# Attention plus token mixer on one core: the softmax sums inverted by way of DRAM, with a new order of score tiles and gelu steps

## The chip, the cores and the metric

The kernel runs on one core of a Trainium2 chip. TensorE (PE) multiplies matrices, VectorE (DVE), ScalarE (ACT) and GpSimd (POOL) work on tiles, and SyncE (SP) issues nearly all DMAs. The metric is the device time in microseconds. "us" below is microseconds.

## The reference, cut to what matters

`x` has 2048 rows and 640 columns. The attention part has 32 heads of 20 columns that share one key and one value matrix. The mixer part works across the rows. A gate per row mixes both.

```
g = sigmoid((x * gate_w).sum(-1, keepdims=True))
q = (x @ wq) in 32 heads of 20;  k = x @ wk;  v = x @ wv
p = softmax(q k^T * 20**-0.5);   a = concat_heads(p @ v) @ wo
h = layernorm(x)
u = gelu(einsum("bsd,sf->bdf", h, w1) + b1)      # F = 1728
b = (einsum("bdf,fs->bds", u, w2) + b2)^T
out = g * a + (1 - g) * b
```

All of it is float32. The kernel keeps the precision by splitting operands into a high and a low part in TensorE's fp32r format and adding three products (high times high, high times low, low times high).

## The kernel before, in words

**Units.** The attention is cut into 32 groups (`NU`), numbered n: four blocks of 512 query rows by eight groups of four heads. Each group has 16 units, one per block of 128 keys. For a unit TensorE makes four score tiles (128 keys by 512 queries, line 702, called "s" here), ScalarE takes the exponential of each (line 711) into a `p` tile, and four matmuls (line 737) multiply the `p` tiles by the values `v_sb`, one head to each 32 rows of one accumulator. The value tile is 20 columns of v and 12 columns of ones, so rows 20 to 31 of each 32-row block of the accumulator hold the softmax sums.

**Row maxima.** Before the exponentials of a group may start, the maximum of each query row must be known. TensorE makes the scores a second time, turned (line 490, called "m"), and VectorE reduces each 128x512 tile to one column (line 496). A group needs 64 m tiles, 32 in each row half of TensorE. The maxima go through a DRAM scratch (lines 523 and 530) into two extra rows of the query tile `qst`. The next group's `qmx` tile is fetched by `new_qmax` (lines 159 and 142: six DMAs) when both halves have started a new group (line 501).

**Stretches.** `main` (line 1085) writes out one stretch: s and m tiles (512 columns, "X") and mixer or projection matmuls (320 columns, "F") on the two row halves of TensorE at the same time, then the value matmuls of two units (`pv_group`, line 727) with the full array. In one half run about 16 X tiles, in the other 15 to 24 F matmuls and one to three X. The two halves change places with each stretch. A group is eight stretches. A table `PATTERN` (line 1060), keyed by the count of F matmuls, gives the order of s and m in the half with the X tiles, and what stands before and after the F matmuls in the other. `share` (line 1068) spreads the m tiles over the stretches: it takes one out of every fourth stretch of the first stage while the table would give more than are needed, and later divides what is left in proportion to the table.

There are three stages of stretches, called here the w1 stage (82 stretches of 24 F, line 993; one more before it fills the pipe), the w2 stage (128 stretches of 20 or 21 F, line 805) and the wo stage (32 stretches of 15 F, line 938). A lead of 46 m tiles per half stands before them and 26 units stand behind them (the tail), where no m tile is left.

**Banks.** Seven PSUM banks serve s, m and the value accumulator. `bank_take` and `bank_give` (lines 456 and 460) choose banks with a small clock of estimated engine times (`USE`, `busy`), which decides the order of the instructions when the program is built.

**The end of a group.** After each pair of units ScalarE copies the accumulator out (line 749), GpSimd adds it to `sums[0]` (line 750). When a group ends (line 751), a list `later` gets steps that `settle` (line 1049) runs one at a time: once in the middle of each stretch, once at its end. A step marked True runs at ends only, unless all row maxima are done (`spare`). Before the change the steps are: `scale` (VectorE turns the 32x32 blocks of `on` into `ot`, line 763, takes the reciprocals of the sums, line 769, and GpSimd multiplies, line 770), `back` (VectorE turns the result back, line 777), `high` (line 780) and `low` (line 783) on GpSimd with eight DMAs of the result to `o_scr` (line 787).

**Queues.** SP issues DMAs in program order and stops at one whose semaphore is not there. Eight DMA semaphores take turns, so a DMA also waits for the eighth before it.

**gelu.** `gelu` (line 534) puts its steps on a list `chain`, of which `settle` runs one at each call (`pop_chain`). In the last line of it (594) are the steps of the 21 columns that run in the w1 stage: `square` on ScalarE, `cube_p` on GpSimd, an empty step, `tanh` on ScalarE, `prod_p` and `high_p` on GpSimd.

**Early loads.** `tail_load(i)` (line 857) fetches rows of `o_scr` and `y_scr` for the tail; line 1042 says in which of the last stretches the first eight are issued.

Of the kernel before, what the change touches and what calls it, by code (L numbers as in the profile page):

```python
# [9 lines left out]
F32 = mybir.dt.float32  # L10
F32R = mybir.dt.float32r
# [6 lines left out]
P = 128  # L18
S, D, H, DH, F = 2048, 640, 32, 20, 1728
# [5 lines left out]
NB = 512  # L25
NQB = S // NB
NQ = H // 4
NU = NQB * NQ
# [12 lines left out]
def mix_kernel(ctx: ExitStack, tc: tile.TileContext, A_x, A_wq, A_wk, A_wv, A_wo,  # L41
               B_x, B_w1, B_b1, B_w2, B_b2, gate_w, out):
    nc = tc.nc
# [9 lines left out]
    o_scr = dram.tile([2, D, S], F32, name="o_scr")  # L53
    y_scr = dram.tile([S, D], F32, name="y_scr")
    m_scr = dram.tile([NU, P, 32], F32, name="m_scr")

    ident = const.tile([P, P], F32, name="ident")
    make_identity(nc, ident)
# [112 lines left out]
    with tc.tile_pool(name="pa", bufs=1) as pa, \  # L171
# [222 lines left out]
        for sb in range(NQB):  # L394
# [11 lines left out]
            for m in range(DC):  # L406
                turned = []
# [59 lines left out]
    def busy(engine, us):  # L467
        clock[engine] = max(clock[engine], clock["now"]) + us
# [65 lines left out]
    def gelu(d, fc, accs):  # L534
        both = fin.tile([P, D], F32, name="yo")
        xg, t1 = both[:, :HD2], both[:, HD2:]
        hi, lo = u_hi[d][:, fc, :], u_lo[d][:, fc, :]
        busy("act", 0.43)
        nc.scalar.activation(xg, accs[0][:, :HD2], AF.Identity, bias=bias[:, NS + fc:NS + fc + 1])

        def square():
            busy("act", 0.38)
            nc.scalar.activation(t1, xg, AF.Square)

        def add():
            nc.vector.tensor_add(xg, xg, accs[1][:, :HD2])  # L546
            square()

        def tanh():
            busy("act", 0.37)  # L550
            nc.scalar.activation(t1, t1, AF.Tanh, scale=GC * 0.044715)

        def high():
            nc.scalar.activation(hi, t1, AF.Copy)

        def low():
            nc.gpsimd.tensor_sub(lo, t1, f32(hi))

        def cube_p():
            nc.gpsimd.tensor_scalar(t1, t1, 1.0, 1.0 / 0.044715, op0=ALU.mult, op1=ALU.add)  # L560
            nc.gpsimd.tensor_mul(t1, t1, xg)

        def prod_p():
            nc.gpsimd.tensor_scalar(t1, t1, 1.0, 1.0, op0=ALU.mult, op1=ALU.add)
            nc.gpsimd.tensor_mul(t1, t1, xg)

        def plus(c):
            nc.scalar.activation(t1, t1, AF.Copy, bias=c)

        def mul():  # L570
            nc.gpsimd.tensor_mul(t1, t1, xg)

        def cubed():
            add()
            plus(1.0 / 0.044715)

        def tanh_plus():
            tanh()
            plus(1.0)

        def high_p():
            nc.gpsimd.tensor_copy(hi, t1)
            nc.gpsimd.tensor_sub(lo, t1, f32(hi))

        if len(accs) == 2:
            ends, ahead[:] = list(ahead), [high, low]
            if fc == PRO - 1:
                add()
                chain.extend((*ends, cube_p, None, tanh, prod_p, high_p))
            else:  # L590
                chain.extend((*ends, *[None] * (2 - len(ends)), cubed, None, None, mul, *[None] * 4, tanh_plus,
                              None, mul, None, None, None))
        else:
            chain.extend((square, cube_p, None, tanh, prod_p, high_p))

    def pop_chain():
        f = chain.pop(0) if chain else None
# [127 lines left out]
    later = []  # L725

    def pv_group(us, keep=False):
        n, kb = units[us[0]]
        assert units[us[-1]][0] == n
        if not otile:  # L730
            otile.append(bank_take())
        o = otile[0]
        opened = not keep or kb == 0 or us[0] == len(units) - TAIL
        ends = kb + len(us) == NS
        for i, u in enumerate(us):
            for hh in range(4):
                nc.tensor.matmul(o[32 * hh:32 * hh + 32, :], v_sb[:, kb + i, :], ptiles.pop((u, hh)),  # L737
                                 start=opened and i == 0, stop=(i == len(us) - 1) and (ends or not keep),
                                 skip_group_check=True)
        if not keep:  # L740
            begin = max(clock["act"], clock["pv"] + 0.14)
            clock["act"] = begin + 0.477
            pool.append((begin + 0.65, otile.pop()))
            if kb == 0:
                sums[0] = ev.tile([P, NB], F32, name="acc", bufs=2)
                nc.scalar.activation(sums[0], o, AF.Copy)
            else:
                part = ev.tile([P, NB], F32, name="part", bufs=2)
                nc.scalar.activation(part, o, AF.Copy)  # L749
                nc.gpsimd.tensor_add(sums[0], sums[0], part)  # L750
        if ends and n < NU - 1:
            qb, g = divmod(n, NQ)
            ot = ev.tile([P, NB // 32, 32], F32, name="ot")
            rl = ev.tile([P, NB // 32], F32, name="rl")
            on = sums[0]
            oh, ol = ot.rearrange("p c e -> p (c e)").bitcast(F32R), on.bitcast(F32R)
            direct = spare[0]
            if keep:
                nc.vector.tensor_add(on, on, o)

            def turn():
                busy("dve", 0.65)
                nc.vector.transpose(ot.rearrange("p c e -> p (c e)"), on)

            def scale():
                if not direct:
                    turn()
                busy("dve", 0.17 if not spare[0] else 0.87)
                nc.vector.reciprocal(rl, ot[:, :, DH])
                (nc.vector if spare[0] else nc.gpsimd).tensor_mul(ot, ot, rl[:, :, None].to_broadcast([P, NB // 32, 32]))  # L770

            if direct:
                turn()

            def back():
                busy("dve", 0.65)
                nc.vector.transpose(on, ot.rearrange("p c e -> p (c e)"))

            def high():
                nc.gpsimd.tensor_copy(oh, on)  # L780

            def low():
                nc.gpsimd.tensor_sub(ol, on, f32(oh))
                for j, t in enumerate((oh, ol)):
                    for hh in range(4):
                        r = (4 * g + hh) * DH
                        nc.sync.dma_start(out=o_scr[j, r:r + DH, qb * NB:(qb + 1) * NB],
                                          in_=f32(t[32 * hh:32 * hh + DH, :]))

            if direct:  # L790
                later.append((False, None))
            later.extend(((True, scale), (True, back), (False, high), (False, low)))

    def b2_jobs(st):
        hold = {}
# [243 lines left out]
    assert sum(visits) == len(units) - TAIL  # L1039
    early = NS - 4 - NA + 4  # L1040
    for i in range(early):
        ph[len(ph) - 3 - 2 * (early - 1 - i)][1].append(lambda i=i: tail_load(i))


    for i, (st, r0, _) in enumerate(jobs):
# [3 lines left out]
    def settle(wide=False):  # L1049
        for _ in range(2 if spare[0] else 1):  # L1050
            if later and (wide or spare[0] or not later[0][0]):
# [5 lines left out]
    sent, back_in = {0}, {0}  # L1057

    AHEAD, DRAIN, ENTER, FIRST = 4, 0.19, 0.138, 0.1
    PATTERN = {24: ("smssmsmmssmssmmm", "Fm"), 20: ("smsmssmmsmmssm", "mFs"), 21: ("smsmsmmssmmsmsm", "Fs"),  # L1060
               15: ("smsssmmmssms", "mFs"), 0: ("mmmmmmmmmmssss", "Fsmm")}

    def pattern(k):
        return PATTERN[len(ph[k][0]) if visits[k] else 0]
# [237 lines left out]
```

## Time and profile before

| | us |
|---|---|
| median of 3 runs (lowest to highest) | 1632.41 (1632.35 to 1633.01) |
| the profiled execution, own time | 1631.96 |
| its span in the profile | 1630.2 |
| DVE busy, share of the span | 1400.5, 86% |
| ACT busy, share of the span | 1297.2, 80% |
| POOL busy, share of the span | 858.5, 53% |
| row maxima on DVE, lines 496 on s and ms banks | 566.1 and 535.9 |
| transposes on DVE, lines 763 and 777, 31 each | 21.8 each |

The span begins with the first instruction that counts and ends with the last; 1.8 us of the run's time lie outside. PE and PEld are TensorE's matmuls and its weight loads. Matmuls of the two row halves overlap in time, and several matmuls are in flight at once, so durations on PE add up to more than passes. In the views of instructions the first column is the start, the second the duration, and "x16" means that rows of the same kind were merged. On DVE and ACT too an instruction starts before the one ahead of it has left: the distance of two starts, and not the duration, is what one costs.

### The profile page before, as it was taken

The numbers are of one execution on the slowest core, as the hardware profiler recorded it, in microseconds if no ns is written. First come the engines' busy times: TensorE is split into PE (matmuls) and PEld (weight loads), VectorE is DVE, ScalarE is ACT, GpSimd is POOL, SyncE is SP. The second block draws the span as 40 slices with busy tenths as digits, with TensorE's granted clock in tenths as the row PEclk, the third lists the DMA queues.
The fourth block names the chain that finished last, engine by engine and source line by source line (L and its number), as shares of the span: only waits on it lengthen the run. The fifth ranks groups of instructions, "written<-read, shape, count | busy, mean of one in ns | idle before, by whom it ended". The sixth has DMA issues, their size and how long they took to land.

```text
span 1630.2 us, 39380 instructions
## 1 busy us (share of the span) xinstructions
PE 1622.6 (100%) x14877; PEld 1127.8 (69%) x14877; DVE 1400.5 (86%) x2404; ACT 1297.2 (80%) x2567; POOL 858.5 (53%) x974
## 2 busy tenths in 40 slices
PE   9999999999999999999999999999999999999998
PEld 7899766766676667666666666666666666666666
DVE  6689999999999999999999999899999999777723
ACT  4445778787887878888888888888888888999975
POOL 6568666767686767544544344354444432433400
PEclk9999999999999999999999999999999999999999
DMA  7655222322233223222212222222222112335421
GB/s 213 210 164 146 71 73 68 74 70 76 70 81 80 63 63 83 57 65 73 65 51 59 58 60 49 73 65 73 65 65 65 54 44 58 95 101 184 133 74 41
DMA packets 173603, 135.88 MB, mean 83 GB/s; under 512 B 32793, under 2 KB 139446, under 8 KB 173414
## 3 DMA queue, kind: packets, MB, share of 16 engines
q1 hardware_dynamic: 173126, 133.04, 29.6%
q8 instruction: 117, 1.92, 0.5%
q14 instruction: 72, 0.59, 0.1%
q10 hardware_dynamic: 288, 0.33, 0.1%
HBM read 100.27 MB, written 31.65 MB: 81 GB/s over the span
## 4 chain that ended last, share of the span: by engine, by line
PE 99%; ACT 0%; DVE 0%; issue 0%; DVEq 0%; ACTq 0%
PE ms L737 14%; PE g L805 11%; PE s L737 11%; PE s L702 9%; PE g L993 9%; PE ms L702 8%; PE ms L490 7%; PE s L490 7%; PE o L737 5%; PE pp L298 4%; PE pu L623 3%; PE o L702 3%; PE o L490 2%; PE g L938 2%; PE ml L490 1%; PE s L893 1%
## 5 line engine op out<-in xcount | busy, mean ns | idle before, releaser
L496 DVE TENSOR_REDUCE mp<-ms 128x1 f32<-128x512 f32 x859 | 566.1, 683 | 69.7 <-PE ms L490 61.9
L496 DVE TENSOR_REDUCE mp<-s 128x1 f32<-128x512 f32 x810 | 535.9, 682 | 44.1 <-PE s L490 37.9
L711 ACT ACTIVATE p<-s 128x512 f32<-128x512 f32 x906 | 534.2, 624 | 37.8 <-PE s L737 13.1
L711 ACT ACTIVATE p<-ms 128x512 f32<-128x512 f32 x847 | 498.3, 621 | 36.7 <-PE s L737 11.4
L750 POOL TENSOR_TENSOR acc<-acc,part 128x512 f32<-128x512 f32 x212 | 274.4, 1294 | 392.9 <-ACT part L749 373.9
L702 PE MATMUL s<-qst,kst 62*128 62x512 f32 x906 | 353.8, 413 | 0.0
L702 PE MATMUL ms<-qst,kst 62*128 62x512 f32 x847 | 335.5, 413 | 0.4 <-ACT p L711 0.4
L490 PE MATMUL ms<-kst,qmx 60*128 60x512 f32 x859 | 332.6, 410 | 0.3 <-ACT p L711 0.3
L490 PE MATMUL s<-kst,qmx 60*128 60x512 f32 x810 | 316.4, 409 | 0.6 <-DVE yo L546 0.5
L993 PE MATMUL g<-slot,wh 64*128 64x320 f32 x1344 | 306.8, 313 | 0.0
L993 PEld LDWEIGHTS g<-slot,wh 64*128 64x128 f32 x1344 | 221.5, 184 | 68.7 <-DVE mp L496 35.2
L129 POOL TENSOR_TENSOR wl<-wr,wh 128x512 fp32r<-128x512 f32 (+1 forms) x176 | 217.7, 1237 | 29.4 <-ACT wh L126 9.7
L737 PE MATMUL ms<-p,v_sb 128*32 128x512 f32 x1904 | 228.9, 598 | 0.0
L496 DVE TENSOR_REDUCE mp<-o 128x1 f32<-128x512 f32 x287 | 196.0, 683 | 20.5 <-PE o L490 18.3
L993 PE MATMUL g<-slot,wl 64*128 64x320 f32 x672 | 206.4, 307 | 0.0
L702 PEld LDWEIGHTS s<-qst,kst 62*128 62x128 f32 x906 | 166.7, 185 | 55.1 <-ACT p L711 31.7
L805 PE MATMUL g<-u,wh 64*128 64x320 f32 x864 | 196.7, 310 | 0.0
L805 PE MATMUL g<-slot,wh 64*128 64x320 f32 x864 | 196.3, 309 | 0.0
L702 PEld LDWEIGHTS ms<-qst,kst 62*128 62x128 f32 x847 | 156.2, 185 | 55.3 <-ACT p L711 43.0
L737 PE MATMUL s<-p,v_sb 128*32 128x512 f32 x1536 | 184.7, 598 | 0.0
L711 ACT ACTIVATE p<-o 128x512 f32<-128x512 f32 x280 | 174.1, 622 | 11.5 <-PE ms L737 5.5
L490 PEld LDWEIGHTS ms<-kst,qmx 60*128 60x128 f32 x859 | 157.5, 185 | 9.2 <-ACT p L711 3.3
(244 smaller groups left out, 3158.0 us busy)
## 6 DMA issues: line engine op xcount, KB each, us to landing
wr<-in_B_w_dram SPq DMA_DIRECT2D x136, 256.0 KB
qmx<-q_scr SPq DMA_DIRECT2D x192, 80.0 KB
qst<-q_scr SPq DMA_DIRECT2D x192, 80.0 KB
y_scr<-yo SPq DMA_DIRECT2D x16, 320.0 KB
slot<-o_scr SPq DMA_DIRECT2D x16, 320.0 KB
o_scr<-ot SPq DMA_DIRECT2D x124, 40.0 KB
o_scr<-acc SPq DMA_DIRECT2D x124, 40.0 KB
q_scr<-qh SPq DMA_DIRECT2D x19, 256.0 KB
```

Source lines behind the costliest of these rows:

```text
L129: nc.gpsimd.tensor_sub(wl[:, :nv], wr[:, :nv], f32(wh[:, :nv]))
L298: nc.tensor.matmul(pp, w, t, start=first and n == 0, stop=not more and n == len(steps) - 1)
L490: nc.tensor.matmul(ms, qmax[n][64 * b:64 * b + 60, pr, qt * P:(qt + 1) * P], kst[64 * b:64 * b + 60, kq * NB:(kq + 1) * NB], start=True, s ...
L496: r = nc.vector.tensor_reduce(mtiles[n][:, c, kq:kq + 1], ms, axis=AX.X, op=ALU.max)
L623: nc.tensor.matmul(pu[r][:, :HD2], w[rows, c, :], h[rows, st, :], start=(st == 0 and k == 0), stop=(st == NS - 1 and k == 2))
L702: nc.tensor.matmul(s, kst[64 * b:64 * b + 62, kb * P:(kb + 1) * P], q[64 * b:64 * b + 62, pr, :], start=True, stop=True)
L711: e = nc.scalar.activation(p, s, AF.Exp, scale=SCALE)
L737: nc.tensor.matmul(o[32 * hh:32 * hh + 32, :], v_sb[:, kb + i, :], ptiles.pop((u, hh)), start=opened and i == 0, stop=(i == len(us) - 1) a ...
L750: nc.gpsimd.tensor_add(sums[0], sums[0], part)
L805: other_tile(half, nc.tensor.matmul(hold["p"][:, :HD2], w[r, i, :], u[d][r, fc, :], start=(hold["n"] == 1), stop=(hold["n"] == 6 * FC - 3)))
L938: other_tile(half, nc.tensor.matmul(hold["p"][:, :HD2], o[r, c, :], w[r, c, d * HD2:(d + 1) * HD2], start=(hold["n"] == 1), stop=(hold["n" ...
L993: other_tile(half, nc.tensor.matmul(hold["p"][:, :HD2], w[r, st % HS, :], h[d][r, st, :], start=(hold["n"] == 1), stop=(hold["n"] == 6 * NS)))
```

## The change

The reciprocals of the sums no longer come from turned tiles. Seven steps replace `scale`, `back`, `high` and `low`, and each runs at the next call of `settle`, at ends and in the middle: `sums_out` (four DMAs of one 2 KB row each, the sums of four heads, to a new DRAM scratch `l_scr`), `sums_in` (one DMA that brings 4 x 512 sums back as 128 rows of 16), `inverse` (VectorE, 128x16, and one DMA of the result to `l_scr`), `inverse_in` (four DMAs, each one head's 512 reciprocals repeated to 32 rows, into `ot`), `scale` (GpSimd multiplies `on` by that in place), then `high` and `low` as before. The one group that ends in the tail with `keep` still uses the two transposes. The table for 24 and for 15 F matmuls is replaced; the one for 15 has four m where it had five. The gelu of the w1 stage waits one more step before `tanh`. The last four of the early loads are issued up to three stretches later.

```diff
+    l_scr = dram.tile([2, NU, 4, NB], F32, name="l_scr")
...
-            chain.extend((square, cube_p, None, tanh, prod_p, high_p))
+            chain.extend((square, cube_p, None, None, tanh, prod_p, high_p))
...
             on = sums[0]
-            oh, ol = ot.rearrange("p c e -> p (c e)").bitcast(F32R), on.bitcast(F32R)
-            direct = spare[0]
+            flat = ot.rearrange("p c e -> p (c e)")
+            oh, ol = flat.bitcast(F32R), on.bitcast(F32R)
             if keep:
                 nc.vector.tensor_add(on, on, o)
 
-            def turn():
-                busy("dve", 0.65)
-                nc.vector.transpose(ot.rearrange("p c e -> p (c e)"), on)
+            def turned():
+                nc.vector.transpose(flat, on)
+                nc.vector.reciprocal(rl, ot[:, :, DH])
+                nc.vector.tensor_mul(ot, ot, rl[:, :, None].to_broadcast([P, NB // 32, 32]))
+
+            def back():
+                nc.vector.transpose(on, flat)
+
+            def sums_out():
+                for hh in range(4):
+                    r = 32 * hh + DH
+                    nc.sync.dma_start(out=l_scr[0, n, hh:hh + 1], in_=on[r:r + 1, :])
+
+            def sums_in():
+                nc.sync.dma_start(out=rl, in_=l_scr[0, n].rearrange("h (r c) -> (h r) c", r=32))
+
+            def inverse():
+                busy("dve", 0.17)
+                nc.vector.reciprocal(rl, rl)
+                nc.sync.dma_start(out=l_scr[1, n].rearrange("h (r c) -> (h r) c", r=32), in_=rl)
+
+            def inverse_in():
+                for hh in range(4):
+                    nc.sync.dma_start(out=flat[32 * hh:32 * hh + 32, :],
+                                      in_=l_scr[1, n, hh:hh + 1].to_broadcast([32, NB]))
 
             def scale():
-                if not direct:
-                    turn()
-                busy("dve", 0.17 if not spare[0] else 0.87)
-                nc.vector.reciprocal(rl, ot[:, :, DH])
-                (nc.vector if spare[0] else nc.gpsimd).tensor_mul(ot, ot, rl[:, :, None].to_broadcast([P, NB // 32, 32]))
-
-            if direct:
-                turn()
-
-            def back():
-                busy("dve", 0.65)
-                nc.vector.transpose(on, ot.rearrange("p c e -> p (c e)"))
+                nc.gpsimd.tensor_mul(on, on, flat)
...
-            if direct:
-                later.append((False, None))
-            later.extend(((True, scale), (True, back), (False, high), (False, low)))
+            first = (None, turned, back) if keep else (sums_out, sums_in, inverse, inverse_in, scale)
+            later.extend((False, f) for f in (*first, high, low))
...
-        ph[len(ph) - 3 - 2 * (early - 1 - i)][1].append(lambda i=i: tail_load(i))
+        ph[len(ph) - (17 - 2 * i if i < early - 4 else 6 + early - 4 - i)][1].append(lambda i=i: tail_load(i))
...
-    PATTERN = {24: ("smssmsmmssmssmmm", "Fm"), 20: ("smsmssmmsmmssm", "mFs"), 21: ("smsmsmmssmmsmsm", "Fs"),
-               15: ("smsssmmmssms", "mFs"), 0: ("mmmmmmmmmmssss", "Fsmm")}
+    PATTERN = {24: ("msmsmmssmsmmsmss", "Fm"), 20: ("smsmssmmsmmssm", "mFs"), 21: ("smsmsmmssmmsmsm", "Fs"),
+               15: ("smsmssmsmss", "mFs"), 0: ("mmmmmmmmmmssss", "Fsmm")}
```

## The prediction

> **What bounds the kernel now.** I read the head of the page first, then busy time by stage, then the timeline of single stretches, engine by engine. The profiled execution took 1631.96 us, of which the span is 1630.2; the median of the three runs, 1632.41, lies 0.45 above it.
>
> ```profile
> span 1630.2 us, 39380 instructions
> ...
> PE 1622.6 (100%) x14877; PEld 1127.8 (69%) x14877; DVE 1400.5 (86%) x2404; ACT 1297.2 (80%) x2567; POOL 858.5 (53%) x974
> ...
> PE 99%; ACT 0%; DVE 0%; issue 0%; DVEq 0%; ACTq 0%
> ```
>
> TensorE is the bound by both its busy share and the chain. But a matmul that waits for a bank counts as busy, so this says which engine, not how much could go. The Trainium skill ("Trainium Kernel Development and Optimization", Performance Expectations) says the same, that matmul busy time is a bad measure and weight-load busy time a good one; by it the 69% of PEld would leave much room. The timeline of the stretches shows less room than that.
>
> The windows are the three stages of stretches (82, 128 and 32 of them):
>
> ```profile
> core 0: us, PE busy (x) PEld busy (x) DVE busy (x) ACT busy (x) POOL busy (x), PEclk, DMA share, GB/s
> 170.70:665.70 495.00, 494.42 (x4662) 344.00 (x4658) 461.61 (x774) 396.43 (x801) 352.61 (x417) 1.00 0.28 72
> 665.70:1384.40 718.70, 718.35 (x6695) 480.65 (x6691) 652.99 (x1106) 612.10 (x1186) 317.62 (x348) 1.00 0.23 61
> 1384.40:1546.50 162.10, 162.10 (x1444) 103.11 (x1440) 124.65 (x211) 152.75 (x304) 66.56 (x72) 1.00 0.43 130
> ```
>
> A stretch costs 495.0/82 = 6.04 us, 718.7/128 = 5.61 us and 162.1/32 = 5.07 us. Next the end of one stretch of the wo stage, on PE:
>
> ```profile
> 1437.53 0.39 PE L490 MATMUL s<-kst,qmx 60*128 60x512 f32 x1
> 1437.61 0.46 PE L702 MATMUL ms<-qst,kst 62*128 62x512 f32 x1
> 1437.87 0.49 PE L702 MATMUL s<-qst,kst 62*128 62x512 f32 x1
> 1438.29 0.64 PE L737 MATMUL ms<-p,v_sb 128*32 128x512 f32 x4
> ```
>
> The X tile at 1437.61 is the last of the half that has the F matmuls. The one at 1437.87 is the twelfth of the other half, and the value matmuls start 0.42 us behind it. So the half with the X tiles sets the end here. And VectorE in the w2 stage, at the end of a group:
>
> ```profile
> 695.45 0.69 DVE L496 TENSOR_REDUCE mp<-ms 128x1 f32<-128x512 f32 x1 [0.83 <-PE ms L490]
> ...
> 700.25 0.70 DVE L763 STREAM_TRANSPOSE ot<-acc 128x512 f32<-128x512 f32 x1
> 700.98 0.25 DVE L769 RECIPROCAL rl<-ot 128x16 f32<-128x16 f32 x1
> 701.23 0.69 DVE L496 TENSOR_REDUCE mp<-s 128x1 f32<-128x512 f32 x1
> ...
> 703.03 0.68 DVE L496 TENSOR_REDUCE mp<-s 128x1 f32<-128x512 f32 x1
> 703.63 0.68 DVE L496 TENSOR_REDUCE mp<-ms 128x1 f32<-128x512 f32 x1
> ...
> 706.02 0.70 DVE L777 STREAM_TRANSPOSE acc<-ot 128x512 f32<-128x512 f32 x1
> ```
>
> Reductions start 0.60 us apart without a break, and between stretches VectorE has one gap (0.83 us of idle time in the first row). The transposes sit in that gap.
>
> **The change part by part.**
>
> *The transposes go.* They cover 0.70 us each, two for each of 30 groups, all in the gap just shown. What is late next without them is again the first m tile of the next stretch. So I count their removal at 0; bounds: 0, and 30 x 2 x 0.60 = 36 us if they were on the path, which the 0.83 us of idle time excludes in the w2 stage.
>
> *Fewer m tiles in the wo stage.* The built program's order has five m where it had six in 21 of the 32 stretches. Of these tiles 18 move to the w1 stage (all 82 stretches have nine, where 18 had eight), one ahead of it, two to the w2 stage. Without its twelfth X tile the one half ends at 1437.53, the other at 1437.61, and the value matmuls can start at 1437.61 + 0.42 = 1438.03, 0.26 earlier. What would be late next is ScalarE, which has as many exponentials as before:
>
> ```profile
> 1433.53 0.59 ACT L952 ACTIVATE yo<-g,g_col 128x320 f32<-128x320 f32 x1
> 1433.94 1.16 ACT L711 ACTIVATE p<-s 128x512 f32<-128x512 f32 x2
> ...
> 1436.23 0.61 ACT L711 ACTIVATE p<-ms 128x512 f32<-128x512 f32 x1
> 1436.71 1.11 ACT L711 ACTIVATE p<-s 128x512 f32<-128x512 f32 x2
> ```
>
> Two starts are 0.48 apart, and line 952 takes 0.41 in every second stretch: 9 x 0.48 + 0.41/2 = 4.53 us in a stretch of 5.07 - 0.26 = 4.81. It fits, but with 4.73 in the stretches that have line 952. I take 0.23 instead of 0.26: 21 x 0.23 = **-4.8 us** (bounds -5.5 and 0).
>
> *The w1 stage.* Starts of the value matmuls of six stretches in a row, the last from another window:
>
> ```profile
> 235.28 1.92 PE L737 MATMUL ms<-p,v_sb 128*32 128x512 f32 x16
> 241.76 1.92 PE L737 MATMUL s<-p,v_sb 128*32 128x512 f32 x16
> 247.77 1.92 PE L737 MATMUL o<-p,v_sb 128*32 128x512 f32 x16
> 253.82 1.92 PE L737 MATMUL s<-p,v_sb 128*32 128x512 f32 x16
> 259.87 1.92 PE L737 MATMUL ms<-p,v_sb 128*32 128x512 f32 x16
> ```
> ```profile
> 265.80 1.50 PE L737 MATMUL s<-p,v_sb 128*32 128x512 f32 x12
> ```
>
> Nine m tiles cost 6.01 to 6.05 us. The first distance, 6.48 us, and the last, 5.93, are stretches of eight; in the first the last m tile waited for a bank. If every stretch took 6.00, the stage would take 492.0, 3.0 less than now. The new table starts with an m, which gives VectorE its first tile one X earlier, and ends in "smss" and not in "mmm", so that fewer banks hang on VectorE when the value matmuls need one. Against that, the nine reductions fill 9 x 0.60 = 5.4 of 6.0 us in each stretch now, and the reciprocal (0.25) stands amid them. I take half: **-1.5 us** (bounds -3.0, and +1.3 if nothing but the 18 added tiles counts, at 6.00 - 5.93 = 0.07 each). The extra gelu step moves `tanh` half a stretch away from `cube_p`, and lies in a chain of eight half stretches; 0.
>
> *The sums through DRAM.* In the w2 stage the built order puts this on SP: four stores of sums, then the **six DMAs of the next `qmx`**, then `sums_in`. VectorE's `inverse` stands behind the fourth reduction of the second stretch after the group's end. All times from T, the first matmul after the group's value matmuls:
>
> ```profile
> 694.89 0.49 PE L702 MATMUL s<-qst,kst 62*128 62x512 f32 x1
> ```
> ```profile
> 695.81 1.29 POOL L750 TENSOR_TENSOR acc<-acc,part 128x512 f32<-128x512 f32 x1 [4.41 <-ACT part L749]
> ```
> ```profile
> 237.57 0.34 SPq L523 DMA_DIRECT2D m_scr<-mt  x1
> 239.30 2.74 SPq L530 DMA_DIRECT2D qst<-m_scr  x4
> ...
> 704.79 2.28 SPq L142 DMA_DIRECT2D qst<-q_scr  x6
> ```
> ```profile
> GB/s 213 210 164 146 71 73 68 74 70 76 70 81 80 63 63 83 57 65 73 65 51 59 58 60 49 73 65 73 65 65 65 54 44 58 95 101 184 133 74 41
> ```
>
> The sum is complete at 697.10, T + 2.2. Four stores at 0.34: SP is free at T + 3.6. The six loads take 2.28 to issue: `sums_in` goes out at T + 5.9. How long it takes to land no row tells. A store of 16 KB is done 239.30 - 237.57 = 1.73 us after its issue (SP waited for it to read it back), which gives T + 7.6 as the lower end. In front of it in the DMA queue stand 6 x 80 KB, 2.25 us at the 213 GB/s of the first slice; if they start to move only when `sums_in` is issued, it lands at T + 9.9. They start up to 2.3 us earlier, so I take T + 8.4, nearer to the lower end. VectorE wants it when the fourth reduction is over, at 703.63, T + 8.7. So VectorE doesn't wait, with 0.3 us to spare. What it would cost: `inverse` would hold the reductions behind it, their banks, and TensorE that waits for these banks. I count **+1.5 us** for the w2 stage, 16 groups x 0.1: the reciprocal's 0.25 now stands amid reductions and no longer in the gap (bounds: 16 x 1.2 = +19 if it lands at T + 9.9, and -2.4, since transpose and reciprocal, 0.98 us together, overran the gap of 0.83 by 0.15 in each group). In the other stages no `qmx` loads stand between (but for two groups), and it lands at T + 2.2 + 1.4 + 2 x 1.73 = T + 7.1 or before, ahead of the middle of the second stretch.
>
> *SP's queue.* SP now stands at the store of the reciprocals until VectorE has run (T + 9.0), and at `inverse_in` for that store (1.73 more). Behind them are two weight loads, a `qst` fetch and the fetch of the maxima. Weights are fetched far ahead, as SP's own waits show, since it stands there for GpSimd to free a buffer; the other two are for the next group, some stretches off: 0.
>
> ```profile
> SPq L110 <- POOL wl L129: 413.1, 29, 28.1
> ```
>
> *Behind the reciprocal.* Its store, `inverse_in` behind up to six loads, and `scale` on GpSimd follow. GpSimd may stand there for some us. It idled 4.41 us before the addition above, its next work is due a stretch later, and nobody waits for `o_scr` until later stages: 0; if it were late, ScalarE's copy of the accumulator two stretches on would wait, at most the 1.3 us of one addition in each group.
>
> *The early loads* move behind the stores that they read; 0.
>
> Sum: -4.8 - 1.5 + 1.5 = -4.8, of 1631.96 that is 1627.2; with the 0.45 to the median **1627.6 us**, 0.3% faster.
>
> **The rivals.**
>
> 1. *VectorE waits for the sums* (slower). The mechanism is the six loads between `sums_out` and `sums_in`; the place is `inverse` in 16 groups of the w2 stage; it decides from T + 8.7 on. For it: 0.3 us of margin on a landing that no row shows. Against it: the loads ahead have two microseconds of head start. Price at a landing of T + 9.6: 16 x 0.9 = +14 against the +1.5 above, so 1640. Beyond 0.2% slower from about 0.6 us of wait. Chance 0.20. The Trainium skill ("DMA: Bandwidth & Descriptors", Specifications) says that pieces below 512 B are read, modified and written; the 64-byte pieces of `sums_in` and of the inverse's store are such. The nearest row, the store of 128-byte pieces above, took 1.73 us; no run here shows 64.
> 2. *The m tiles only change their place.* The wo stage stays at 5.07 since ScalarE, at 4.73 of 4.81, and not the X tiles, sets its end (0), the w1 stage lies between -1.5 and +1.3, the w2 stage at +1.5: 1632.4 to 1635.2, say 1633. For it: ACT busy 152.75 of 162.10 there. Chance 0.20.
> 3. *It gives more than the forecast.* Every stretch of the w1 stage at 6.00 (-3.0), wo at -5.5, the w2 stage -2.4: 1632.4 - 10.9 = 1621.5. For it: VectorE gets the gap back in all stages. Against it: the w2 stage has hardly a stretch that shows it missing. Chance 0.10.
> 4. *The change doesn't do what it says*: the transposes still run, since `keep` groups use them. Only one group is such. Chance 0.
>
> **How the numbers follow.** Forecast 0.50, rivals 0.20, 0.20, 0.10. The range reaches from the third rival, 1621.5, to the first with 0.65 us of wait, 1637; beyond lie about 0.15 on the upper and 0.04 on the lower side. 0.2% is 3.3 us, about what a measurement of this kernel can tell from no change. Faster than 1629.1: most of the forecast (0.46) and rival 3, 0.56. Within: 0.04 of the forecast and most of rival 2, 0.21. Slower than 1635.7: rival 1 and the rest, 0.23.
>
> **What would show it.** Stretches of five m tiles in the wo stage at 4.8 to 4.85 us (right) or 5.0 and more (rival 2). The w1 stage at 492 to 495. In the w2 stage no idle time of VectorE before its new reciprocal; if "DMA" appears there as the releaser with over 0.5 us a time, rival 1 holds and the stage is longer than 720. GpSimd waiting at `scale`, without a trace on PE. The forecast fails where the landing is misjudged, or where another of TensorE's waits for banks comes up under the new table.

## The result, and the profile after

| | us |
|---|---|
| before, median of 4 runs beside it (lowest to highest) | 1632.38 (1632.18 to 1633.01) |
| after, median of 4 runs (lowest to highest) | 1625.18 (1623.61 to 1627.24) |
| ratio, 95% interval | 0.9956 (0.9944 to 0.9969) |
| profiled execution of after, own time and span | 1627.24 and 1625.4 |

The kernel is faster by 7.2 us, 0.4%. The forecast was 1627.6, in the range and 2.4 us too high. The changed kernel's runs differ by 3.6 us, those of before by 0.8, and the profiled execution is the slowest of the four. In after, lines from 490 to 760 are numbered one higher than before (L703 is the s tile, L491 m, L497 its reduction, L738 the value matmul); L773 stores the sums, L776 loads them, L780 is the new reciprocal, L781 its store, L785 loads the repeated rows, L789 is GpSimd's multiply, and the F matmuls of the three stages are L1004, L816 and L949.

The head of the page of after, busy times and chain:

```profile
span 1625.4 us, 39511 instructions
...
PE 1616.6 (99%) x14877; PEld 1127.4 (69%) x14877; DVE 1351.8 (83%) x2344; ACT 1311.0 (81%) x2567; POOL 866.6 (53%) x974
...
PE 97%; DMA 1%; SPq 1%; DVE 1%; ACT 0%; POOL 0%; issue 0%; DVEq 0%; ACTq 0%; POOLq 0%
```

VectorE has 49 us less work. New in the chain are DMA, SP's queue and VectorE, 1% each, where TensorE had 99%: something that TensorE waits for now comes through DRAM. The same three stages as before, and the tail, with the columns of the windows in the prediction:

```profile
172.00:662.40 490.40, 490.24 (x4678) 347.24 (x4674) 452.95 (x773) 410.79 (x801) 354.88 (x418) 1.00 0.30 79
662.40:1383.70 721.30, 720.52 (x6695) 480.13 (x6691) 630.58 (x1075) 613.37 (x1186) 323.61 (x350) 1.00 0.24 67
1383.70:1541.40 157.70, 156.82 (x1423) 99.68 (x1419) 106.34 (x180) 150.60 (x304) 64.43 (x66) 1.00 0.46 137
1541.40:1614.20 72.80, 72.42 (x744) 48.80 (x740) 20.79 (x38) 50.42 (x101) 7.78 (x10) 1.00 0.17 53
```

The w1 stage is 4.6 us shorter (495.0 before), the w2 stage 2.6 longer (718.7), the wo stage 4.4 shorter (162.1), the tail 0.8 longer (72.0). The w1 stage begins 1.3 us later than before; behind the tail 0.5 is saved. Sum: -4.8, the difference of the spans. Starts of value matmuls, two neighbours in the w1 stage, then two in the wo stage:

```profile
253.91 1.92 PE L738 MATMUL ms<-p,v_sb 128*32 128x512 f32 x16
259.86 1.92 PE L738 MATMUL ms<-p,v_sb 128*32 128x512 f32 x16
```
```profile
1429.76 1.92 PE L738 MATMUL ms<-p,v_sb 128*32 128x512 f32 x16
1434.55 1.93 PE L738 MATMUL ms<-p,v_sb 128*32 128x512 f32 x16
```

5.95 us with nine m tiles in the w1 stage (6.01 to 6.05 before), 4.79 with five in the wo stage (5.07 with six). A stretch is timed here from one start of value matmuls to the next, and named by the value matmuls that open it; the prediction counted from T, the end of a group's last value matmuls, so its second stretch is the first behind a group here. In the w2 stage the usual stretch is what it was, but the second stretch behind some groups takes up to 6.6 us. One such place in the chain of waits (start, duration):

```profile
1318.60 1.85 PE ms L738 x16
...
1325.68 0.99 SPq L143
...
1326.77 3.82 DMA rl<-l_scr
...
1330.62 0.25 DVE rl L780
1330.87 2.34 DVE mp L497 x4
...
1333.26 0.41 PE s L703
```

and the same time in SP's and VectorE's timelines:

```profile
1322.63 1.11 SPq L773 DMA_DIRECT2D l_scr<-acc  x4
1323.83 2.84 SPq L143 DMA_DIRECT2D qmx<-q_scr  x6
1326.77 0.35 SPq L776 DMA_DIRECT2D rl<-l_scr  x1
```
```profile
1330.62 0.25 DVE L780 RECIPROCAL rl<-rl 128x16 f32<-128x16 f32 x1 [1.41 <-DMA rl<-l_scr]
```

SP stores the sums, issues six `qmx` loads, and only then the load of the sums. That lands 3.82 us after its issue, VectorE stands 1.41 us at the reciprocal, four reductions come late, and TensorE waits for their banks. In all, from the waits:

```profile
DVE rl L780 <- DMA rl<-l_scr: 6.5, 8, 1.4
```

Eight groups, 6.5 us. Seven of them are in the w2 stage, 0.8 us a time, and the stage is longer than 720: by the prediction's own sign that is rival 1. The eighth is at the end of the wo stage. GpSimd waits far longer at its multiply, as the view of that line shows (sum in us, times):

```profile
its engine sat idle before it (us, times) until:
  DMA qst<-m_scr: 62.0, 17
  DMA ot<-l_scr: 28.6, 10
  DMA m_scr<-mt: 8.0, 2
  DMA qmx<-q_scr: 2.7, 1
```

101 us, in all of its 30 groups. The tile it reads is `ot`; that the other names are loads which landed in the same moments is argued, not shown.

### The profile page after: what moved, and what is told of

Its sections match the earlier page's. It is cut to its first block, busy times and chain, and to the rows that moved or that the text cites. A ratio compares the mean times of both kernels' runs of the same rounds, so it can differ in the third digit from the quotient of the medians.

```text
span 1625.4 us, 39511 instructions
## 1 busy us (share of the span) xinstructions
PE 1616.6 (99%) x14877; PEld 1127.4 (69%) x14877; DVE 1351.8 (83%) x2344; ACT 1311.0 (81%) x2567; POOL 866.6 (53%) x974
## 4 chain that ended last, share of the span: by engine, by line
PE 97%; DMA 1%; SPq 1%; DVE 1%; ACT 0%; POOL 0%; issue 0%; DVEq 0%; ACTq 0%; POOLq 0%
PE ms L738 18%; PE g L816 11%; PE ms L703 9%; PE g L1004 9%; PE s L703 9%; PE s L738 8%; PE s L491 7%; PE ms L491 5%; PE pp L299 4%; PE pu L624 3%; PE o L703 3%; PE o L738 2%; PE o L491 2%; PE g L949 2%; PE ml L491 1%; PE ms L904 1%
## 5 line engine op out<-in xcount | busy, mean ns | idle before, releaser
L497 DVE TENSOR_REDUCE mp<-s 128x1 f32<-128x512 f32 x910 | 595.0, 679 | 91.1 <-PE s L491 76.8
L712 ACT ACTIVATE p<-ms 128x512 f32<-128x512 f32 x940 | 542.4, 616 | 47.5 <-PE s L738 17.5
L497 DVE TENSOR_REDUCE mp<-ms 128x1 f32<-128x512 f32 x748 | 493.6, 679 | 58.7 <-PE ms L491 45.5
L712 ACT ACTIVATE p<-s 128x512 f32<-128x512 f32 x813 | 474.7, 612 | 36.4 <-PE ms L738 10.6
L491 PE MATMUL s<-kst,qmx 60*128 60x512 f32 x910 | 366.1, 417 | 0.6 <-DVE yo L547 0.5
L703 PE MATMUL ms<-qst,kst 62*128 62x512 f32 x940 | 359.7, 408 | 0.3 <-ACT part L750 0.2
L703 PE MATMUL s<-qst,kst 62*128 62x512 f32 x813 | 325.1, 412 | 0.4 <-ACT p L712 0.2
L1004 PE MATMUL g<-slot,wh 64*128 64x320 f32 x1344 | 306.4, 312 | 0.0
L738 PE MATMUL ms<-p,v_sb 128*32 128x512 f32 x2544 | 305.9, 598 | 0.0
L491 PE MATMUL ms<-kst,qmx 60*128 60x512 f32 x748 | 296.3, 411 | 0.0
L1004 PEld LDWEIGHTS g<-slot,wh 64*128 64x128 f32 x1344 | 216.8, 184 | 68.7 <-issue 54.5
L497 DVE TENSOR_REDUCE mp<-o 128x1 f32<-128x512 f32 x298 | 202.4, 679 | 22.1 <-PE o L491 16.0
L1004 PE MATMUL g<-slot,wl 64*128 64x320 f32 x672 | 205.3, 305 | 0.0
L703 PEld LDWEIGHTS ms<-qst,kst 62*128 62x128 f32 x940 | 171.8, 185 | 48.2 <-ACT p L712 24.7
L703 PEld LDWEIGHTS s<-qst,kst 62*128 62x128 f32 x813 | 150.1, 185 | 72.6 <-ACT p L712 41.6
L816 PE MATMUL g<-slot,wh 64*128 64x320 f32 x864 | 197.4, 310 | 0.0
L816 PE MATMUL g<-u,wh 64*128 64x320 f32 x864 | 196.7, 309 | 0.6 <-POOL wh L129 0.6
L491 PEld LDWEIGHTS s<-kst,qmx 60*128 60x128 f32 x910 | 166.3, 185 | 7.3 <-DVE mp L497 1.7
L738 PEld LDWEIGHTS ms<-p,v_sb 128*32 128x32 f32 x2544 | 66.4, 109 | 135.1 <-issue 95.2
```

What stands on the lines that cost most here:

```text
L491: nc.tensor.matmul(ms, qmax[n][64 * b:64 * b + 60, pr, qt * P:(qt + 1) * P], kst[64 * b:64 * b + 60, kq * NB:(kq + 1) * NB], start=True, s ...
L497: r = nc.vector.tensor_reduce(mtiles[n][:, c, kq:kq + 1], ms, axis=AX.X, op=ALU.max)
L703: nc.tensor.matmul(s, kst[64 * b:64 * b + 62, kb * P:(kb + 1) * P], q[64 * b:64 * b + 62, pr, :], start=True, stop=True)
L712: e = nc.scalar.activation(p, s, AF.Exp, scale=SCALE)
L816: other_tile(half, nc.tensor.matmul(hold["p"][:, :HD2], w[r, i, :], u[d][r, fc, :], start=(hold["n"] == 1), stop=(hold["n"] == 6 * FC - 3)))
L1004: other_tile(half, nc.tensor.matmul(hold["p"][:, :HD2], w[r, st % HS, :], h[d][r, st, :], start=(hold["n"] == 1), stop=(hold["n"] == 6 * NS)))
```

## The experiments

Stage times in us, each from a window of the trace that begins and ends with a stage's last value matmuls:

| | w1 | w2 | wo | tail | median, us |
|---|---|---|---|---|---|
| before | 495.0 | 718.7 | 162.1 | 72.0 | 1632.4 |
| e1 tables alone | 494.9 | 723.8 | 156.6 | 72.2 | 1632.44 |
| e5 tables and gelu step | 492.3 | 723.2 | 156.8 | 72.1 | 1629.18 |
| e2 all but the tables | 493.1 | 716.3 | 163.8 | 75.5 | 1630.59 |
| e6 all but the gelu step | 504.1 | 723.8 | 158.1 | 73.1 | 1644.91 |
| after | 490.4 | 721.3 | 157.7 | 72.8 | 1625.18 |
| e3 sums stored and loaded in one step | 490.8 | 723.5 | 157.8 | 72.9 | 1625.79 |
| e4 and a later reciprocal | 495.9 | 768.6 | 156.9 | 72.0 | 1681.95 |
| e7 one trip, reciprocal of the whole tile | 525.6 | 763.2 | 162.5 | 72.1 | 1708.60 |
| e8 no normalisation | 489.1 | 719.1 | 156.6 | 72.0 | 1621.42 |
| e9 later multiply | 489.7 | 719.5 | 157.6 | 73.6 | 1624.58 |
| e10 e3 and later multiply | 489.7 | 717.2 | 157.7 | 72.9 | 1622.47 |
| e11 e10 without the gelu step | 494.9 | 718.5 | 157.9 | 73.2 | 1628.62 |
| e12 e10, reciprocal later too, end by transposes | 488.7 | 718.7 | 157.3 | 72.0 | 1621.53 |

Each row's stage times are of the one profiled execution, whose own time is not the median: that of e3 is 4.2 us above its median, those of after and e2 are 2 above, that of e6 is 1.4 below and that of e4 4.4 below.

**e1, e2: tables, and the rest without them.** e1 is the kernel before with

```diff
-    PATTERN = {24: ("smssmsmmssmssmmm", "Fm"), 20: ("smsmssmmsmmssm", "mFs"), 21: ("smsmsmmssmmsmsm", "Fs"),
-               15: ("smsssmmmssms", "mFs"), 0: ("mmmmmmmmmmssss", "Fsmm")}
+    PATTERN = {24: ("msmsmmssmsmmsmss", "Fm"), 20: ("smsmssmmsmmssm", "mFs"), 21: ("smsmsmmssmmsmsm", "Fs"),
+               15: ("smsmssmsmss", "mFs"), 0: ("mmmmmmmmmmssss", "Fsmm")}
```

and e2 is the kernel after with the reverse of that.

> Only the two new tables for 24 and 15 F matmuls; the sums are still inverted by way of VectorE's transposes. Theory (the tables bring the gain, the route by DRAM brings none): the w1 stage at 5.95 to 5.97 us a stretch, the stretches of five m tiles in the wo stage at 4.8, no wait in the w2 stage: 1621 to 1623 us. Rival (the tables only work because VectorE lost its transposes): VectorE, with nine m tiles in each stretch of the w1 stage, stalls TensorE where the transposes stand, and the time is 1626 to 1630.

> Only the route by DRAM, the gelu step and the early loads; the tables of before. In this order the six qmx loads don't stand between sums_out and sums_in. Theory: nothing is gained, since the transposes stood in VectorE's gap, and the reciprocal amid the reductions costs about 0.1 us in each group: 1632 to 1635. Rival (transposes were what held TensorE): 1626 to 1629.

e1: 1632.44 (1631.75 to 1632.66), ratio 0.9999 (0.9990 to 1.0008). e2: 1630.59, ratio 0.9991 (0.9983 to 1.0000). The theory that the tables alone bring the gain fell, and e1 is also slower than its rival's 1626 to 1630; e2 lies between its two forecasts. The tables' own 5.5 us in the wo stage are there, but the w1 stage gains nothing and the w2 stage loses 5.1. In the w1 stage of e1 the stretches take 5.96 us like those of after, but every fourth one takes 6.2. Value matmuls, and then ScalarE ahead of the late ones:

```profile
260.60 1.92 PE L737 MATMUL s<-p,v_sb 128*32 128x512 f32 x16
```
```profile
266.80 1.50 PE L737 MATMUL s<-p,v_sb 128*32 128x512 f32 x12
```
```profile
264.88 0.59 ACT L711 ACTIVATE p<-ms 128x512 f32<-128x512 f32 x1
265.36 0.47 ACT L551 ACTIVATE yo<-yo 128x320 f32<-128x320 f32 x1
265.72 0.60 ACT L711 ACTIVATE p<-ms 128x512 f32<-128x512 f32 x1
```

`tanh` (L551) stands between exponentials that the value matmuls wait for. In after it stands behind them, 0.7 us after the value matmuls have begun (5.95 behind 259.86):

```profile
266.54 0.51 ACT L552 ACTIVATE yo<-yo 128x320 f32<-128x320 f32 x1
```

The w2 stage of e1 has 5.84 us in the second stretch behind each group, where 5.57 is usual. The tables shift the row maxima against the groups, and VectorE's small steps for the maxima (L511, L522) now meet the transposes (L763, L777) in the two gaps:

```profile
700.99 0.20 DVE L511 TENSOR_REDUCE mm<-mp 128x16 f32<-128x64 f32 x1
701.12 0.70 DVE L763 STREAM_TRANSPOSE ot<-acc 128x512 f32<-128x512 f32 x1
...
706.75 0.70 DVE L777 STREAM_TRANSPOSE acc<-ot 128x512 f32<-128x512 f32 x1
707.38 0.17 DVE L522 STREAM_TRANSPOSE mt<-mn 128x32 f32<-128x32 f32 x1
```

In e2 there are few such stalls: the w2 stage gains 2.4 us, the w1 stage 1.8, and the tail loses 3.5. That loss is one stretch of 8.9 us where 5.4 is usual: GpSimd stands 4.21 us at the last trip's multiply, the steps for the last row maxima (L514 to L516) stand behind it, VectorE stands for those, and TensorE for VectorE. The same place takes 6.2 us in after.

**e5, e6: the gelu step.** e5 is e1 with the extra empty step, e6 the kernel after without it:

```diff
-            chain.extend((square, cube_p, None, None, tanh, prod_p, high_p))
+            chain.extend((square, cube_p, None, tanh, prod_p, high_p))
```

> The kernel before with both new tables and with the extra empty gelu step, but with its own transposes. Theory (the tables' gain in the w1 stage needs the gelu step: with the tables alone tanh stands in the middle of every fourth stretch and delays an exponential, 0.25 us in some 20 stretches): the w1 stage falls from the tables' 494.9 us to about 490.5, the w2 stage keeps the tables' 723.8, the time falls from 1632.4 to about 1627.5 to 1629. Rival (the stall in every fourth stretch comes from VectorE's transposes or from the tables themselves): w1 stays at 494 to 495 and the time at 1631.5 to 1632.5.

> The kernel after without the extra gelu step. Theory (the step is worth what the stall in every fourth stretch costs): the w1 stage rises from 490.4 us to about 494 to 495, the time from 1625.2 to about 1629 to 1630. Rival (without transposes VectorE has room enough that tanh's place does not matter): 1625 to 1626.

e5: 1629.18 (1628.45 to 1629.49), ratio 0.9980 (0.9971 to 0.9988), 0.2 us above what was expected, and the w1 stage is at 492.3 and not 490.5: the stretches of 6.2 in every fourth place are gone, but the first behind each group takes 6.2 to 6.4, and in after, without transposes, 6.06. e6: 1644.91 (1643.49 to 1648.73), ratio 1.0084 (1.0071 to 1.0098). The direction was expected, not the size, 19.7 us where some 5 were: one stretch of its w1 stage takes 12.4 us from end to end of its value matmuls. That place in the trace of e6, GpSimd first, then ScalarE, then windows of 4 us:

```profile
284.24 1.29 POOL L789 TENSOR_TENSOR acc<-acc,ot 128x512 f32<-128x512 f32 x1 [6.97 <-DMA m_scr<-mt]
...
293.13 0.86 POOL L562 TENSOR_TENSOR yo<-yo 128x320 f32<-128x320 f32 x1
```
```profile
294.02 0.47 ACT L552 ACTIVATE yo<-yo 128x320 f32<-128x320 f32 x1 [4.41 <-POOL yo L562]
```
```profile
290.00:294.00 4.00, 0.75 (x6) 0.30 (x2) 1.99 (x4) 0.00 (x0) 3.83 (x6) 1.00 0.40 102
294.00:298.00 4.00, 2.97 (x13) 0.78 (x17) 0.69 (x1) 2.42 (x5) 3.83 (x5) 0.67 0.38 86
298.00:302.00 4.00, 4.00 (x42) 3.06 (x34) 2.51 (x5) 2.79 (x6) 3.92 (x5) 0.90 0.32 78
```

GpSimd stood 6.97 us at the multiply. Behind it in its queue stand 7 us of casts, splits and additions and then the cube (L561, L562) for `tanh`; ScalarE stands 4.41 us at `tanh`, the exponentials stand behind that, and TensorE is busy for 0.75 of 4 us. So the new trip couples GpSimd's queue to ScalarE, and the extra gelu step gives the cube half a stretch more.

**e3, e4: where the trip's time goes.** e3 is the kernel after with the store and the load in one step, so that the `qmx` loads stand behind both; in e4 the reciprocal also runs one step later, and high and low run in one step.

```diff
+            def both():
+                sums_out()
+                sums_in()
-            first = (None, turned, back) if keep else (sums_out, sums_in, inverse, inverse_in, scale)
+            first = (None, turned, back) if keep else (both, None, inverse, inverse_in, scale)
...
+            def split():
+                high()
+                low()
+            first = (None, turned, back, high, low) if keep else (both, None, None, inverse, inverse_in, scale, split)
```

> The changed kernel with sums_in in the same step as sums_out, so that it is ahead of the qmx loads on SP. Theory (VectorE waits for the sums behind these loads): VectorE's wait for rl goes from 7.1 us to under 1, the long stretches of the w2 stage go, that stage is back at 717 to 719, and the time is 1620 to 1622.5. Rival (the stalls in the w2 stage come from more DMA traffic or from the two stretches with nine m tiles): the stage stays at 721 and the time at 1624 to 1626.

> As e3, and the reciprocal moved to the end of the second stretch, into VectorE's gap; high and low run in one step. Theory: besides what e3 gains, the 0.1 us of the second stretch after each group's end goes in the w1 stage, 10 times: 1619 to 1621.5. Rival (the 0.1 us has another cause): same as e3.

Both expectations failed. e3: 1625.79 (1625.08 to 1629.99), ratio 0.9965 (0.9953 to 0.9978), in the range of its rival's time. VectorE no longer waits, but for 0.9 us once in the wo stage, and now the third stretch behind a group is the long one. Its chain at such a place:

```profile
746.97 0.17 DVE rl L780
...
747.15 5.42 DMA l_scr<-rl
...
754.78 2.18 DMA ot<-l_scr
...
757.09 1.29 POOL acc L789
...
759.05 0.46 POOL wh L129
...
759.55 0.41 PE g L820
```

The store of 8 KB takes 5.42 us behind the bulk loads, GpSimd multiplies late, and behind that stands the split of the next weights (L129), for which TensorE's F matmul (L820 here) waits. e4, where the reciprocal's store stands behind the six `qst` loads too, shows the same at full size: 1681.95, ratio 1.0299 (1.0285 to 1.0313), and in its waits

```profile
PEld g L824 <- POOL wh L129: 34.3, 16, 4.1
```

So it is not VectorE alone that pays: GpSimd's wait reaches TensorE through the weights.

**e7, e8: one trip, and none.** e7 takes the reciprocal of the whole 128x512 tile and makes one trip instead of two: the rows of reciprocals go out and come back repeated. e8 leaves the five steps out, so its output lacks the division by the sums.

```diff
-            first = (None, turned, back) if keep else (sums_out, sums_in, inverse, inverse_in, scale)
+            first = (None, turned, back) if keep else (None, inverse, inverse_in, None, scale)
...
+            first = (None, turned, back) if keep else (None, None, None, None, None)
```

> The kernel after with one trip through DRAM in place of two: at the end of the first stretch behind the group VectorE takes the reciprocal of the whole 128x512 tile, the four rows of reciprocals are stored, and the repeated rows are read back half a stretch later. VectorE waits for no DMA, and GpSimd's multiply has more time. Theory (what the change loses in the w2 stage is VectorE's wait for the sums and GpSimd's wait for the reciprocals): the stretches of 6 us and more in the w2 stage go, the stage falls from 721.3 us to 716 to 717, the time to 1619.5 to 1621.5. Rival (the full reciprocal costs VectorE what the transposes cost under these tables, 0.27 us in each of 16 stretches): the w2 stage stays at 720 to 724, the time at 1624 to 1627.

> The kernel after without the normalisation of its groups: the five steps from the store of the sums to GpSimd's multiply are left out (the output lacks the division by the sums for all groups but the last; high and low run where they ran). This is what the rest of the change gives when the route costs nothing. Theory: w2 stage about 716, time 1618.5 to 1620.5, so the route costs the changed kernel 5 to 6 us. Rival (the 6 us stretches have another cause, such as the qmx loads): w2 stays at 720 to 721, time 1624 to 1625.

e7 failed: 1708.60, ratio 1.0469 (1.0454 to 1.0483). Its groups of instructions tell why:

```profile
L772 DVE RECIPROCAL ot<-acc 128x512 f32<-128x512 f32 x30 | 100.2, 3340 | 0.0
```

3.34 us for 512 columns, where 16 columns take 0.25: a reciprocal costs some 6.2 ns a column ((3340 - 250) / 496), and the tile nearly five times a transpose. e8: 1621.42 (1621.18 to 1622.00), ratio 0.9935 (0.9923 to 0.9948). By the medians e8 is 3.8 us below the changed kernel, less than the 5 to 6 expected, and its w2 stage is at 719.1 where about 716 was expected. The stretch before each group's last takes 5.69 us there, as before the change, and 5.59 in after: 1.6 us in the stage. So e8 is no floor, and 3.8 us need not be the whole price of the trip.

**e9, e10: time for GpSimd.** e9 is the kernel after with the multiply one stretch later; e10 is e9 with the store and load in one step as in e3.

```diff
-            first = (None, turned, back) if keep else (sums_out, sums_in, inverse, inverse_in, scale)
+            first = (None, turned, back) if keep else (sums_out, sums_in, inverse, inverse_in, *((None, None) if n < NU - 3 else ()), scale)
...
+            first = (None, turned, back) if keep else (both, None, inverse, inverse_in, *((None, None) if n < NU - 3 else ()), scale)
```

> The kernel after with GpSimd's multiply (and high and low behind it) one stretch later, two empty steps ahead of it, for all groups but the last ones; VectorE's reciprocal stands where it stood. GpSimd's wait for the repeated reciprocals is covered, VectorE's wait for the sums is not. Theory (in the kernel after it is VectorE that pays, GpSimd's wait costs little): the long stretches of the w2 stage, the second behind each group, stay, w2 at 719.5 to 721.5, time 1623 to 1625. Rival (GpSimd's wait is what costs): w2 at 716 to 718, time 1619 to 1621.

> The same later multiply, and the store and the load of the sums in one step as in the experiment with both together, so that the six qmx loads stand behind both. Both waits are covered. Theory (the two waits are all that the route costs): no stretch of the w2 stage over 5.8 us but those of nine m tiles, w2 at 716 to 717, w1 at 489 to 490, time 1618.5 to 1620.5, that of the kernel without the normalisation or below, and faster than the kernel after by 5 to 6 us. Rival (the chain of four DMA hops is delayed elsewhere, as the store of the reciprocals was by 5 us, and the bulk loads behind it in SP's queue come late): 1622 to 1626.

e9: 1624.58 (1622.83 to 1625.28), ratio 0.9950 (0.9937 to 0.9964); time and w2 stage (719.5) are in the range of its theory, that GpSimd's wait costs little. e10: 1622.47 (1621.35 to 1623.43), ratio 0.9940 (0.9928 to 0.9953), 2 us over what was expected and in the range of its rival, since the end did not gain: the last groups were left as they were, and the wo stage and the tail still hold 2 us over e8. The w2 stage is near what was expected: 717.2, and no stretch over 5.8 us but two with nine m tiles and the stage's first (5.99). GpSimd's waits in e10:

```profile
its engine sat idle before it (us, times) until:
  DMA m_scr<-mt: 3.5, 1
  DMA ot<-l_scr: 3.2, 1
  DMA qst<-m_scr: 1.4, 1
```

101 us have become 8. From after to e9 (GpSimd's wait covered) the w2 stage falls by 1.8 us and the w1 stage by 0.7; from e9 to e10 (VectorE's too) the w2 stage by 2.3. With GpSimd's wait left, e3, the latter brings nothing. But the execution of after is its slowest, and VectorE's waits differ between the two as well. Three stretches of after behind long waits of GpSimd show its price alone: 6.67 us for 5.96 (w1 stage), 6.60 for 5.99 and 5.80 for 5.57 (w2 stage), 1.5 us in all. By the medians e9 is 0.6 us below after, which the intervals don't tell from nothing, and e10 2.7 below, every run of it below every run of after.

**e11, e12.** e11 is e10 without the gelu step. e12 is e10 with

```diff
+            first = (None, turned, back) if keep or n >= NU - 3 else (both, None, None, inverse, inverse_in, None, None, None, scale)
```

> The kernel with both waits covered (the later multiply, sums stored and loaded in one step), but without the extra gelu step. Taken from the changed kernel, that step's loss cost 19.7 us, half of it in the w1 stage, where tanh stood behind a cube that GpSimd could not begin while it stood at the multiply. Theory (the step protects ScalarE from GpSimd's wait, so with the wait covered only tanh's place in every fourth stretch is left, 0.25 us in some 20 stretches of the w1 stage): w1 at 494 to 496, w2 at 717 to 718, time 1626 to 1629. Rival (the step's worth has nothing to do with GpSimd's wait): w1 at 500 to 505, time 1638 to 1643.

> The kernel with both waits covered, with the reciprocal at the end of the second stretch behind the group instead of its middle, the multiply one and a half stretches after that of the changed kernel's place to leave room for it, and with the last but one group by the two transposes. Theory (in the w1 stage the reciprocal in the middle of a stretch costs 0.11 us, 10 times, since VectorE has no room inside a stretch but has some at its end; the two stalls near the tail come from the last groups' trip): w1 at 488.7 to 489.2, w2 at 717, wo stage and tail 2 us less, time 1619 to 1621. Rival (at the stretch's end the reciprocal delays the next stretch's first maxima just as much, and the chain behind it is late): 1622 to 1626.

e11: 1628.62 (1627.63 to 1628.99), ratio 0.9978 (0.9969 to 0.9987), as expected: with GpSimd's wait covered the gelu step is worth 6.2 us, and not 19.7. e12: 1621.53 (1621.24 to 1622.17), ratio 0.9936 (0.9924 to 0.9949), half a microsecond over the expectation, by its median the fastest kernel with the whole computation, and level with e8. The w1 stage (488.7) and the tail (72.0) came out as expected; the wo stage gained only 0.4 us. The w2 stage gave 1.5 us back: with the reciprocal between stretches, the stretch before each group's last takes 5.68 us again, as before the change and in e8; why is open.

## Why the prediction came out as it did

The bound (TensorE, by waits for banks) was right. The time was near, by errors that cancel: own time 1627.2 was forecast and 1627.24 measured, but that execution is the slowest of four, 2 us above the median, and the three stages moved by -6.4 where -4.8 was forecast; the other +1.6 (start, tail, end) stood in no term. So the close hit is in part luck. The terms were these.

- *Transposes, 0.* Near enough for the old order (e2, without them but with the trip and the gelu step, is 1.8 us faster), wrong for the new one, and that is where the step failed: "The transposes sit in that gap" was read off the old trace, and the tables put other work of VectorE into the same gap (e1: 0.27 us in each group of the w2 stage). Without transposes, e5 against after, the w1 stage gains 1.9 more.
- *wo stage, -4.8.* Measured -4.4. The mechanism was right, and the 0.03 us a stretch taken off for ScalarE was not needed (5.07 to 4.79 is 0.28; rival 2 fell). e1 shows the whole of it, -5.5; after gives about 1 us back where the last groups' trips end.
- *w1 stage, -1.5, at best -3.0.* Measured -4.6. The term was mis-sized: the floor is 5.95 and not 6.00. And it needs the gelu step, which was counted at 0: e10 against e11, 5.2 us in this stage. The working looked at the distance of `tanh` from `cube_p` and not at which exponentials ScalarE has to hold back.
- *Sums through DRAM, +1.5.* The w2 stage as a whole measured +2.6. Six stretches behind late reciprocals are together 3.1 us longer than the usual 5.57; against that, the stretch before each group's last is 0.10 shorter than before, 1.6 us that no term held. The place and mechanism of rival 1 are in the chain: the load of the sums was issued at 1326.77, 6.3 us behind T (value matmuls of 1.85 us from 1318.60, so T is 1320.45; 5.9 was forecast), and it landed at T + 10.1, beyond the upper end of T + 9.9, while VectorE wanted it at T + 8.8 (8.7 forecast). So "VectorE doesn't wait" failed. But only seven groups of the stage were late, so rival 1's price of 14 us did not come.
- *Behind the reciprocal, 0.* This failed in kind. GpSimd stood at the multiply, as the text said it might, but "nobody waits" looked at `o_scr` and the addition alone. In GpSimd's queue behind it stand the gelu's cube, for ScalarE, and the weights, for TensorE. Price 1.5 us in the stages of after (the three stretches above) and 0.7 in its tail, and some 45 us where the chain is longer still (w2 stage of e4 less that of e3; e4 also runs high and low in one step).
- *The early loads, 0*: e12, which has them, has the tail of before (72.0). *SP's queue, 0*: not tried by itself; e10, which lets SP stand at the same places, has no long stretch left in the w2 stage.

What follows for the change itself: the three parts need one another. Each against the kernel before measured beside it: tables alone 0.0, with the gelu step -3.1, with the trip too -7.2; tables and trip without the gelu step +12.6; trip and step without tables -1.8. The early loads came with the trip each time.

The Trainium skill ("DMA: Bandwidth & Descriptors", Latency and other measured facts) says that the fixed cost of a DMA of about 2 us is mostly the latency of its target memory, and that it grows with the load. The trace agrees in kind: 8 KB took 3.82 and 5.42 us above, each time behind or beside loads of 80 KB, so a sum of minimal landings does not price a chain of four. No run here tells a slower memory from waiting behind those loads.

## What to carry to other kernels

Where a step is moved from one engine to a chain of DMAs, list what stands behind each waiting instruction in its own engine's queue, down to the engine that sets the time, and give every engine that waits for a link slack: here slack for GpSimd and VectorE together was worth 2.7 us, and for either alone nothing that stood clear of the noise (e9, e3). What a shorter chain is worth is not shown, since the one tried (e7) lost by VectorE's time. Read a gap as free only in the order that will run: an edit which packs the bound engine tighter also moves other engines' small steps into the gaps that hid something. Where parts of a change bring little alone, try them in pairs before explaining any one of them.

## What was not expected of the hardware

VectorE's reciprocal costs 3.34 us for 128x512 and 0.25 for 128x16, by these two points about 6.2 ns a column, against 0.70 us for a transpose of the same tile. After 4.28 us in which TensorE did nothing in e6 (from 290.75 to 295.03; the first window above has 0.75 of 4 us busy), the granted clock was 0.67 in the window 294 to 298 and 0.90 in the 4 us behind it, so a stall costs more than its own length. From 296 to 298 it was 0.50. An estimate from these three: half speed for 3.4 us ((0.33 + 0.10) x 4 / 0.5). The Trainium skill ("TensorE: Matmul & The Clock Gate", Part 1: The HAM clock gate) states the rule: half rate after an idle window of about 3.4 us, until a window of work of the same length. The trace agrees: idle for 4.28 us, then half speed for about 3.4.
